# A scheduled one-core kernel: state powers in two halves, first loads in order of use, masks on either engine

## The chip, the cores and the metric

The kernel runs on one core of a Trainium2 chip. The metric is device time in microseconds; the kernel before has a median of 374.18 us over three runs (372.81 to 378.39). The engines are named as the profile names them: PE (TensorE, matrix products), PEld (its weight loads), DVE (VectorE), ACT (ScalarE), POOL (GpSimd) and SP (SyncE, which here only issues transfers). A transfer is issued on the queue of SP, ACT or POOL and carried out by 16 DMA engines.

## The reference

A block of 2048 tokens and 512 channels gets two treatments, and a gate per token mixes them.

```python
def _A_ref(x, wq, wk, wv, wo, beta):          # attention in 4 segments of 512 tokens, 32 heads of 16
    q, k, v = ...                             # x @ wq, x @ wk, x @ wv, by heads and segments
    for s in range(4):
        logits = einsum('bhqd,bhkd->bhqk', qs, ks) * scale + mask      # causal mask
        p = _softmax(logits)
        a_dot = einsum('bhqk,bhkd->bhqd', p, vs)
        num, den = phi(qs) @ M, phi(qs) @ z + 1e-06                    # memory of earlier segments
        o = g * (num / den) + (1.0 - g) * a_dot
        M, z = M + phi(ks)^T vs, z + sum(phi(ks))
    return o @ wo

def _B_ref(u, A_re, A_im, B_re, B_im, C_re, C_im, log_dt, Dskip):      # a long convolution per channel
    logdA, dB = dt * (A_re + 1j * A_im), dt * (B_re + 1j * B_im)       # 512 channels x 128 states
    P = exp(logdA[:, :, None] * l[None, None, :])                      # powers for l = 0..2047
    K = einsum('dn,dnl,dn->dl', Cc, P, dB).real
    return irfft(rfft(u) * rfft(K)) + u * Dskip

g = _sigmoid((x * gate_w).sum(-1))
return g * _A_ref(...) + (1 - g) * _B_ref(x, ...)
```

(Shortened: reshapes, casts and padding are left out.)

## The kernel before

The kernel records all its operations in a list, and a list scheduler of its own, at build time, puts them in an order for each engine, with a rough cost of each operation and a priority: a base key by stage plus an offset by tag, from a table (`ORDER`). The engines then run their fixed lists, with semaphores between them. Operations that copy a PSUM or SBUF tile (`evac`) may go to ACT or DVE, as the scheduler finds it best. All transfers, matrix products and evacuations have one line of code each (L295, L805, L302 and L303), so tiles and sizes tell them apart, not lines.

The parts that matter here:

First loads. Constants and parameters go on SP's queue; x of the first segment and the projection weights (`early`) are issued by ACT at its start.

```python
prm = (B_A_re, B_A_im, B_B_re, B_B_im, B_C_re, B_C_im)
for wi in range(6):                                  # 128 KB each, in rows of 256 bytes
    S.dma(ap(T, dims=[[128, 4], [1, 128]]), prm[wi].rearrange("(k p) n -> p k n", p=128), ..., key=0.1 * wi - 1)
S.dma(ldt, B_log_dt, ..., key=-0.9)
for T, wsrc, ky in ((wqT, A_wq, 0.3), (wkT, A_wk, 0.4), (wvT, A_wv, 0.5), (woT, A_wo, 9.0)):
    S.dma(..., 524288, w=[T], key=ky, early=ky < 1)
```

Preparation. The parameters are transposed on PE (L866), exp(dt A) is built by DVE and ACT as a real and an imaginary part, `zr` and `zi` (128 states x 512 channels, fp32).

Powers. Ten squarings give the powers 1, 2, 4, ... 512; each is stored in bf16 as re, re, im, -im, and all 512 channels are handled at once:

```python
for k in range(10):
    ACT.activation(pwT[re, re], zr, Copy)                       # L904, 128x1024
    ACT.activation(pwT[im], zi, Copy)                           # L906, 128x512
    DVE.tensor_scalar(pwT[-im], pwT[im], -1.0, mult)            # L908
    ACT: s_ = Square(zr);  d_ = Square(zi)                      # L914, L915
    DVE: ni = 2 * zr * zi                                       # L916
    DVE: nr = s_ - d_                                           # L917
    zr, zi = nr, ni
    if k == 5: ssm_cb(pb, dt)                                   # coefficients C * dt * B, 8 DVE products of 512
```

Tables. For each of four blocks of 128 channels, products of powers (L1286, L1288, L1291, DVE) build two tables, whose matrix product gives the kernel K at the exponents needed.

Attention. For each segment and group of four heads in a quarter there are five score tiles of 128x1024: score products, a causal mask, then an exponential on ACT (L1151, 160 in all). The mask is either added by one more matrix product (`negm`) before the exponential or multiplied on DVE after it (L1160); which of the two is fixed by the group:

```python
md = 8 * s + 2 * hg + gi >= MASKD            # MASKD = 24: groups 24..31 on DVE, the others on PE
...
i = mm(e, ap(PV, 128 * J, n=n, p0=32 * c, np_=17), ap(vpad[s], J * 544 + (8 * hg + hh) * 17, n=17),
       ap(pT, bk * 512 + off, n=n), ...)     # value products: 16 values and a one per head
```

Spectral stage. x is transformed in two levels, K in one (matrix products with constants), and for 16 steps the products (L1383, L1385, L1388 on DVE) and the inverse products follow. The block of a step is moved by one transfer of 256 KB into `V2`. At the end 16 products of 512 columns join the two branches, an evacuation with the gate as a scale (L305 on ACT, L306 on DVE) follows each, and the output goes out in four stores of 512 KB:

```python
for gq in range(4):
    for bl in range(4):
        pre = b4 < 4                          # the first four banks get the attention branch ahead
        ...
        S.evac(ou[bl * 512], P, 512, scale=omg4T[b4])
    S.dma(out[gq], ou, 524288)
```

Of the kernel before, what the change touches and what calls it, by code (L numbers as in the profile page):

```python
# [15 lines left out]
WIN = 3.4133  # L16
WARM = -1.0
ORDER = {
    '': (-173.582, -53.129), 'ld0': (-114.93, -18.308), 'ld1': (-97.586, 12.303), 'ld2': (-314.483, -141.787),
    'ld3': (-17.474, -40.663), 'ld4': (-139.345, 38.763), 'ld5': (-76.269, -93.461), 'ldt': (-233.997, 43.095),  # L20
    'ldw': (86.442, 71.281), 'ldc': (138.223, -52.008), 'prep': (-61.363, -40.369), 'xT': (45.662, 7.703),
    'pow0': (-321.882, -76.587), 'pow1': (-126.209, -27.757), 'pow2': (-371.748, 4.435), 'pow3': (-150.147, -151.241),
    'pow4': (-80.653, -40.547), 'pow5': (3.774, -97.638), 'cb': (-251.329, 15.495), 'pow6': (-117.016, -94.946),
    'pow7': (-462.139, 36.763), 'pow8': (-33.623, -108.583), 'pow9': (-299.842, -83.973), 'gate': (22.932, 16.612),
    'proj0.0': (-110.151, -32.513), 'tok0': (-116.048, -20.841), 'state0': (15.373, 156.393),
    'grp0.0.0': (32.669, 0.046), 'grp0.0.1': (29.753, -16.453), 'oph0.0': (63.818, -280.473),
    'proj0.1': (16.198, -92.393), 'grp0.1.0': (50.038, 50.955), 'grp0.1.1': (50.606, 0.038),
    'oph0.1': (57.101, -360.883), 'proj0.2': (-64.871, 8.032), 'grp0.2.0': (21.522, 77.803),
    'grp0.2.1': (-7.319, 72.147), 'oph0.2': (43.593, -240.036), 'proj0.3': (-113.204, -26.034),
    'grp0.3.0': (-78.183, 33.502), 'grp0.3.1': (28.034, -5.119), 'oph0.3': (-89.886, -294.08),  # L30
    'oproj0': (76.822, 66.15), 'proj1.0': (-17.113, -10.461), 'tok1': (6.274, 31.316), 'state1': (-1.66, 138.163),
    'grp1.0.0': (-244.675, -22.146), 'grp1.0.1': (-80.842, -7.868), 'oph1.0': (-51.814, -311.307),
    'proj1.1': (7.334, 23.195), 'grp1.1.0': (-94.814, 24.193), 'grp1.1.1': (83.913, -51.668),
    'oph1.1': (-151.77, -343.043), 'proj1.2': (33.686, -22.884), 'grp1.2.0': (-69.387, -48.159),
    'grp1.2.1': (-184.853, 63.024), 'oph1.2': (-146.431, -298.02), 'proj1.3': (-92.277, -78.378),
    'grp1.3.0': (-54.416, 120.304), 'grp1.3.1': (-52.668, 43.268), 'oph1.3': (-174.49, -380.844),
    'oproj1': (7.311, -29.399), 'proj2.0': (24.317, 2.404), 'tok2': (24.751, -29.031), 'state2': (-46.584, 38.683),
    'grp2.0.0': (-351.626, -1.006), 'grp2.0.1': (-94.412, 115.243), 'oph2.0': (69.419, -267.27),
    'proj2.1': (54.998, 38.92), 'grp2.1.0': (-252.693, -101.772), 'grp2.1.1': (-113.295, 30.139),
    'oph2.1': (-75.116, -437.037), 'proj2.2': (25.433, -57.215), 'grp2.2.0': (209.043, -22.16),  # L40
    'grp2.2.1': (-134.171, 67.883), 'oph2.2': (-117.243, -224.354), 'proj2.3': (217.053, -66.312),
    'grp2.3.0': (-116.791, -42.427), 'grp2.3.1': (13.259, 57.3), 'oph2.3': (143.136, -318.104),
    'oproj2': (-82.069, 10.995), 'proj3.0': (-162.313, -44.706), 'tok3': (-80.971, -45.086),
    'grp3.0.0': (-214.436, 3.177), 'grp3.0.1': (-101.384, -2.77), 'oph3.0': (40.647, -200.262),
    'proj3.1': (22.37, -26.764), 'grp3.1.0': (-25.243, 111.691), 'grp3.1.1': (-28.3, -75.051),
    'oph3.1': (-322.009, -418.76), 'proj3.2': (133.931, 42.56), 'grp3.2.0': (-51.289, -21.993),
    'grp3.2.1': (-62.933, 19.274), 'oph3.2': (153.415, -361.736), 'proj3.3': (139.126, -24.669),
    'grp3.3.0': (-204.609, 17.588), 'grp3.3.1': (-19.033, 89.621), 'oph3.3': (-9.379, -316.322),
    'oproj3': (141.911, 55.366), 'tab0': (-1.318, 68.48), 'tab1': (-14.305, 103.702), 'tab2': (17.704, 166.03),
    'tab3': (9.574, 76.971), 'xl1': (-178.257, -77.81), 'tailload': (299.499, -81.655), 'K0': (12.758, -9.76),  # L50
    'K1': (23.5, 113.643), 'K2': (-132.789, 127.457), 'K3': (-95.002, 49.886), 'K4': (-85.344, 60.314),
    'K5': (43.411, 19.376), 'K6': (39.014, 116.102), 'K7': (-22.501, 110.737), 'K8': (127.362, 73.851),
    'K9': (51.648, 57.67), 'K10': (-209.146, 67.286), 'K11': (-205.063, 112.443), 'K12': (-128.947, -8.718),
    'K13': (4.27, 178.298), 'K14': (-92.042, 99.167), 'K15': (163.434, 25.732), 'fin': (-79.92, 127.658),
    'fin0': (-437.293, 23.203), 'fin1': (-241.427, 81.848), 'fin2': (-232.803, 71.759), 'fin3': (-355.442, 133.346),
}
MASKD = 24
# [113 lines left out]
class Op:  # L171
    __slots__ = ("eng", "cost", "fn", "deps", "key", "tiles", "wt", "nd", "succ", "start", "fin", "idx", "inc",
                 "val", "sem", "know", "waits", "seq", "lat", "alld", "tag", "alts", "pen", "early", "act", "dma")


class Sched:
# [57 lines left out]
    def op(self, eng, cost, fn, r=(), w=(), pw=(), key=None, lat=None, acq=(), alts=None, act=0.0):  # L234
        o = Op()
# [6 lines left out]
        o.dma = False  # L242
        o.act = act
# [56 lines left out]
    def evac(self, dst, src, n, r, w=(), pw=(), key=None, scale=None, psum16=False, sb=False):  # L300
        if scale is None:
            fa = lambda e: e.activation(dst(), src(), ACT.Copy)  # L302
            fd = lambda e: e.tensor_copy(dst(), src())  # L303
        else:
            fa = lambda e: e.activation(dst(), src(), ACT.Copy, scale=scale())  # L305
            fd = lambda e: e.tensor_scalar(dst(), src(), scale(), None, ALU.mult)  # L306
        ex = 0.09 if scale is not None else 0.0
        return self.op("ANY", 0.0, None, r=r, w=w, pw=pw, key=key,
                       alts={"ACT": (0.17 + 0.000833 * n + ex, fa), "DVE": (0.15 + (0.00026 if sb else 0.00052 if psum16 else 0.00104) * n + ex / 2, fd)})


    def schedule(self):
# [23 lines left out]
        dma_free = 0.0  # L336
        gate = [0.0, 0.0, False]
# [12 lines left out]
        while nleft:  # L350
# [72 lines left out]
            elif e == "PE":  # L423
                left, x = o.cost, est
                while est >= gate[0] + WIN:
                    gate[2] = gate[1] > WARM * WIN
                    gate[0] += WIN
                    gate[1] = 0.0
                while left > 1e-9:
                    sp = 1.0 if gate[2] else 0.53  # L430
                    we = gate[0] + WIN
                    can = (we - x) * sp
                    d_ = min(left, can)
                    gate[1] += d_ / o.cost * o.act
                    if can >= left:
                        x += left / sp
                        left = 0.0
                    else:
                        left -= can
                        x = we  # L440
                        gate[2] = gate[1] > WARM * WIN
                        gate[0] = we
                        gate[1] = 0.0
                t[e] = x
                o.fin = x + 0.05
            else:
                t[e] = est + max(0.05, o.cost - (0.1 if e != "POOL" else 0.0))
                o.fin = est + o.cost
# [206 lines left out]
def build_kernel(nc, A_x, A_wq, A_wk, A_wv, A_wo, A_beta, B_A_re, B_A_im, B_B_re, B_B_im,  # L655
                 B_C_re, B_C_im, B_log_dt, B_Dskip, gate_w, out):
    with contextlib.ExitStack() as es:
# [20 lines left out]
        pidx = np.arange(128)  # L678
        ident = cload(np.eye(128), "ident", BF16, -2)
        mkT = cload((pidx // 16) % 2 == 1, "mk", F32, 4)  # L680
        negm = cload(np.where(pidx[None, :] < pidx[:, None], NEG, 0.0), "negm", BF16, 5)
        mask01 = cload(pidx[None, :] >= pidx[:, None], "mask01", BF16, 8)
# [3 lines left out]
        bdT = cload(bd, "bd", F32, 8)  # L686
        onesT = cload(np.ones((128, 2)), "ones", BF16, 9)
        W1T = cload(W1c, "W1", BF16, 9)
        G2T = cload(G2c, "G2", BF16, 9)
# [46 lines left out]
        vpP = mkpool("vpad", 4352, 2)  # L736
# [21 lines left out]

        a = T1
        pbP = mkpool("pb", 1024, 6, 0)  # L760
        Tp = a
        prP = mkpool("pr", 1024, 6, -1)
        a = Tp
        ftP = mkpool("ft", 2048, 7, 0)
        assert a <= T2, (a, T2)
        a = T2
        dtP = mkpool("dt", 1024, 1, 0)
        ldP = mkpool("ld", 1024, 1, 0)
        assert a <= 207 * 1024, a
# [40 lines left out]
        for wi in range(6):  # L810
            T = Tile(prP, BF16)
            S.tag = "ld%d" % wi
            S.dma(lambda T=T: ap(T, dims=[[128, 4], [1, 128]]), lambda wi=wi: prm[wi].rearrange("(k p) n -> p k n", p=128),
                  131072, w=[T], key=0.1 * wi - 1)
            praw.append(T)
        ldt = Tile(ldP, BF16)
        S.tag = "ldt"
        S.dma(lambda: ap(ldt, n=512), lambda: bass.AP(B_log_dt, 0, [[0, 128], [1, 512]]), 131072, w=[ldt], key=-0.9)
        S.tag = "ldw"
        for T, wsrc, ky in ((wqT, A_wq, 0.3), (wkT, A_wk, 0.4), (wvT, A_wv, 0.5), (woT, A_wo, 9.0)):  # L820
# [37 lines left out]
        def ssm_prep():  # L858
# [20 lines left out]
            def ft():  # L879
                return Tile(ftP, F32)  # L880
# [638 lines left out]
```

## Time and profile before

The profiled execution took 371.05 us, 369.3 us from its first to its last instruction.

| what | number |
|---|---|
| median of three runs | 374.18 us |
| PE busy | 306.9 us, 83% |
| DVE busy | 290.2 us, 79% |
| ACT busy | 288.8 us, 78% |
| granted PE clock, mean | 0.949 |
| read from HBM, written | 20.63 MB, 7.86 MB |
| 160 exponentials (L1151) | 155.7 us on ACT |
| all evacuations of PSUM and copies on ACT (L302), on DVE (L303) | 85.6 us, 69.6 us |

A row of the table of groups names line, engine, operation, the tiles and the shape of one instruction with its count, then busy time in us and the mean of one in ns, then the idle time before it and what ended it. A stretch of the table by stage gives for each engine how much of it was busy. Idle time of an engine counts only where the end waits for it.

### The profile page before, as it was taken

The numbers are of one execution on the slowest core, as the hardware profiler recorded it, in microseconds if no ns is written. First come the engines' busy times: TensorE is split into PE (matmuls) and PEld (weight loads), VectorE is DVE, ScalarE is ACT, GpSimd is POOL, SyncE is SP. The second block draws the span as 40 slices with busy tenths as digits, with TensorE's granted clock in tenths as the row PEclk, the third lists the DMA queues.
The fourth block names the chain that finished last, engine by engine and source line by source line (L and its number), as shares of the span: only waits on it lengthen the run. The fifth ranks groups of instructions, "written<-read, shape, count | busy, mean of one in ns | idle before, by whom it ended". The sixth has DMA issues, their size and how long they took to land.

```text
span 369.3 us, 8529 instructions
## 1 busy us (share of the span) xinstructions
PE 306.9 (83%) x3583; PEld 133.9 (36%) x3583; DVE 290.2 (79%) x636; ACT 288.8 (78%) x373; POOL 20.2 (5%) x38
## 2 busy tenths in 40 slices
PE   0477464998998988999888998999998999999593
PEld 0333111334444344334454343443332354434231
DVE  2268999999699998999865997389787789897310
ACT  2179999899899876888875988899868698446454
POOL 2010000000000010100300000000020200100000
PEclk9989955799999999999999999999999999999878
DMA  6910100111320135714402003000454733433414
GB/s 196 221 57 2 59 0 2 57 59 68 105 79 0 59 128 191 211 65 172 141 19 62 2 2 114 19 5 3 148 185 126 242 111 112 136 101 112 114 75 170
DMA packets 21413, 34.41 MB, mean 93 GB/s; under 512 B 8864, under 2 KB 13984, under 8 KB 20512
## 3 DMA queue, kind: packets, MB, share of 16 engines
q1 hardware_dynamic: 16112, 16.58, 14.4%
q0 software_dynamic: 3152, 15.21, 12.2%
q10 hardware_dynamic: 2112, 2.10, 1.7%
q8 instruction: 28, 0.46, 0.5%
q14 instruction: 9, 0.07, 0.1%
HBM read 20.63 MB, written 7.86 MB: 77 GB/s over the span
## 4 chain that ended last, share of the span: by engine, by line
DVE 46%; PE 30%; ACT 16%; DMA 3%; issue 2%; SPq 2%
PE psum L805 29%; DVE sb L303 9%; DVE sb L1288 8%; DVE sb L1291 7%; DVE sb L1286 6%; ACT sb L1151 5%; ACT sb L302 3%; ACT sb L305 2%; DMA sb<-in_B_A_re_dram 2%; ACT sb L904 2%; DVE sb L1198 2%; SPq L295 2%; DVE sb L1218 2%; DMA sb<-sb 1%; DVE sb L1160 1%
## 5 line engine op out<-in xcount | busy, mean ns | idle before, releaser
L805 PE MATMUL psum<-sb 128*32 128x20 bf16 (+16 forms) x3319 | 289.7, 272 | 39.3 <-ACT sb L1151 12.0
L805 PEld LDWEIGHTS psum<-sb 128*128 128x128 bf16 (+6 forms) x3319 | 117.4, 95 | 206.0 <-issue 69.2
L1151 ACT ACTIVATE sb<-psum 128x1024 bf16<-128x1024 f32 x160 | 155.7, 1030 | 8.2 <-PE psum L805 6.8
L302 ACT ACTIVATE sb<-psum 128x512 bf16<-128x512 f32 (+4 forms) x113 | 85.6, 771 | 53.3 <-PE psum L805 44.0
L303 DVE CAST sb<-psum 128x512 bf16<-128x512 f32 (+2 forms) x77 | 62.1, 813 | 15.1 <-PE psum L805 14.8
L1286 DVE TENSOR_TENSOR sb<-sb 128x512 bf16<-128x512 bf16 (+3 forms) x52 | 35.4, 683 | 0.2
L1288 DVE TENSOR_TENSOR sb<-sb 128x512 bf16<-128x512 bf16 (+3 forms) x52 | 34.5, 680 | 0.0
L1291 DVE TENSOR_TENSOR sb<-sb 128x512 bf16<-128x512 bf16 (+3 forms) x52 | 33.3, 653 | 0.2
L1160 DVE TENSOR_TENSOR sb<-sb 128x512 bf16<-128x512 bf16 (+1 forms) x40 | 14.1, 361 | 3.3 <-ACT sb L1151 3.2
L303 DVE COPY sb<-psum 128x1024 bf16<-128x1024 bf16 (+1 forms) x8 | 4.7, 582 | 13.0 <-PE psum L866 13.0
L305 ACT ACTIVATE sb<-psum,sb 128x512 bf16<-128x512 f32 x14 | 9.2, 687 | 7.0 <-PE psum L805 7.0
L866 PE MATMUL psum<-sb 128*128 128x128 bf16 x24 | 3.0, 309 | 13.9 <-DMA sb<-in_B_A_re_dram 13.9
L1388 DVE TENSOR_TENSOR sb<-sb 128x512 bf16<-128x512 bf16 x32 | 13.1, 417 | 0.4
L295 POOL DMA_DIRECT2D sb<-c_D x16 | 8.6, 538 | 87.9 <-PE psum L805 86.2
L1385 DVE TENSOR_TENSOR sb<-sb 128x1024 bf16<-128x1024 bf16 x16 | 11.0, 685 | 2.2 <-ACT sb L302 2.1
L1383 DVE TENSOR_TENSOR sb<-sb 128x1024 bf16<-128x1024 bf16 x16 | 10.8, 686 | 1.7 <-PE psum L805 1.2
L904 ACT ACTIVATE sb<-sb 128x1024 bf16<-128x1024 f32 x10 | 10.6, 1059 | 0.5 <-DVE sb L917 0.5
L1198 DVE TENSOR_TENSOR sb<-psum,sb 128x512 bf16<-128x512 bf16 x16 | 10.8, 681 | 0.0
L295 POOL DMA_DIRECT2D sb<-in_A_x_dram x7 | 4.7, 671 | 104.4 <-PE psum L848 33.5
L1190 PE MATMUL psum<-sb 128*128 128x128 bf16 x128 | 9.8, 220 | 0.5 <-DVE sb L303 0.5
L303 DVE COPY sb<-sb 128x256 bf16<-128x256 bf16 x13 | 2.8, 290 | 8.7 <-PE psum L805 8.7
L1218 DVE TENSOR_TENSOR sb<-psum,sb 128x256 bf16<-128x256 f32 x24 | 9.3, 410 | 0.2
(78 smaller groups left out, 164.7 us busy)
## 6 DMA issues: line engine op xcount, KB each, us to landing
sb<-c_D POOLq DMA_DIRECT2D x16, 320.0 KB, 3.6
scr_Z<-sb SPq DMA_DIRECT2D x16, 256.0 KB, 2.0
sb<-scr_Z POOLq DMA_DIRECT2D x4, 1024.0 KB, 5.2
sb<-sb SPq DMA_DIRECT2D x16, 256.0 KB
sb<-in_A_x_dram POOLq DMA_DIRECT2D x7, 512.0 KB, 4.5
out_dram<-sb SPq DMA_DIRECT2D x4, 512.0 KB, 3.0
scr_abuf<-sb SPq DMA_DIRECT2D x12, 128.0 KB, 1.8
sb<-scr_abuf SPq DMA_DIRECT2D x3, 512.0 KB, 4.2
```

The costliest lines, as they stand in the source:

```text
L295: o = self.op(q, 0.05 if early else issue if q == "SP" else 1.1, lambda e: e.dma_start(out(), in_(), **kw), r=r, w=w, pw=pw, key=key, lat= ...
L302: fa = lambda e: e.activation(dst(), src(), ACT.Copy)
L303: fd = lambda e: e.tensor_copy(dst(), src())
L805: mm = lambda e, o_, l, r_, st, sp, **kw: e.matmul(o_, lhsT=l, rhs=r_, start=st, stop=sp, skip_group_check=True, **kw)
L904: op("ACT", c_act(1024) + 0.04, lambda e, k=k, zr=zr: e.activation(ap(pwT[0], k * 512, [[5120, 4], [128, 2], [1, 128]]), ap(zr, 0, [[128, ...
L1151: op("ACT", c_act(1024), lambda e, P=P, pT=pT: e.activation(ap(pT, n=1024), ap(P, n=1024), ACT.Exp, scale=0.25), r=[P], w=[pT])
L1160: op("DVE", c_tt(128 * len(offs)), lambda e, pT=pT, dims=dims: e.tensor_tensor(ap(pT, dims=dims + [[1, 128]]), ap(pT, dims=dims + [[1, 128]]),
L1198: op("DVE", c_dps(512), lambda e: e.tensor_tensor(ap(o1, dims=[[128, 4], [16, 8], [1, 16]]), ap(P, dims=[[256, 4], [32, 8], [1, 16]]), ap( ...
L1218: op("DVE", c_dps(256), lambda e, hb=hb: e.tensor_tensor(ap(o2, hb * 256, [[128, 2], [16, 8], [1, 16]]), ap(P2, hb * 512, [[136, 2], [17, ...
L1286: op("DVE", c_tt(256 * n), lambda e: e.tensor_tensor(run(tile, ne, dst, 1), run(tile, ne, src, sstep), pwv(0), ALU.mult), r=rd + [pw], w=w ...
L1288: op("DVE", c_tt(256 * n), lambda e: e.tensor_tensor(run(t2, n, 0, 1), run(tile, ne, src, sstep), pwv(1), ALU.mult), r=rd + [pw], w=[t2])
L1291: op("DVE", c_tt(256 * n), lambda e: e.tensor_tensor(D_(), D_(), ap(t2, n * 128, [[-n * 128, 2], [2 * n, 64], [1, 2 * n]]), ALU.add), r=[t ...
```

## The change

It changes five things, and with them the whole table of priorities.

- Loads: all first loads go through SP's queue, each with a tag of its own, so that their order can be set by use. The parameters are read in rows of 1 KB (four channels per partition, put right by the evacuation after the transposes), x of the first segment in two halves.
- Powers: the ten squarings are done for channels 0 to 255 (A) and 256 to 511 (B) apart. Real and imaginary part lie in one tile, so one square of 512 and one copy of 512 serve both; the copies and the square may go to ACT or DVE. Half B has a later key. Coefficients are made in halves too.
- Value products write 32 columns per head instead of 17, so that the rows between are written as well; the padding is set to zero.
- Masks: a table says for each of the 160 score tiles whether PE or DVE does its mask.
- End: the last block goes in two transfers, six banks get the attention branch ahead instead of four, and the output goes out in six stores of 256 KB and four of 128 KB.

In the scheduler the model of PE's clock is dropped, and transfers are taken to begin at 4.5 us.

```diff
-MASKD = 24
+MASKS = [0, 0, 0, 0, 28, 0, 0, 31, 4, 0, 18, 20, 7, 4, 1, 0, 0, 5, 29, 26, 16, 21, 23, 0, 8, 8, 30, 30, 31, 21, 12, 8]
...  (ORDER: all offsets differ; tags for single loads and for powA0..9, powB0..9, cbA, cbB, gate0, pre0, pre1 are new)
-            S.dma(lambda T=T: ap(T, dims=[[128, 4], [1, 128]]), lambda wi=wi: prm[wi].rearrange("(k p) n -> p k n", p=128),
-                  131072, w=[T], key=0.1 * wi - 1)
+            S.dma(lambda T=T: ap(T, n=512), lambda wi=wi: prm[wi].rearrange("(p k) n -> p (k n)", k=4),
+                  131072, w=[T], key=(-1.3, -1.4, 3.0, 3.1, 3.2, 3.3)[wi])
...
-                  524288, w=[T], key=ky, early=ky < 1)
+                  524288, w=[T], key=ky)
...
+            for hb in (range(2) if s == 0 else (None,)):
+                S.dma(lambda ...: ap(xks, hb * 1024, dims=[[512, n], [1, 512]]), ...,
+                      131072 * n, w=[xp[-1]], key=(-1.2 + 0.1 * hb if s == 0 else S.key - 8), q="SP" if s == 0 else "POOL")
...
-        def ssm_powers(pb, dt, zr, zi):
+        def ssm_powers(pb, dt, z, hf):
             for k in range(10):
-                (ACT copies of 1024 and 512, DVE negation of 512)
+                S.evac(dst(128, 2), ap(z, dims=[[128, 2], [256, 2], [1, 128]]), 512, sbf=True)
+                op("DVE", c_ts4(256), tensor_scalar(dst(384, 1), dst(256, 1), -1.0, None, ALU.mult))
+                S.evac(dst(0, 1), dst(128, 1), 256, sb=True)
-                (ACT squares of 512 twice, DVE products of 512 twice)
+                op("ANY", ..., alts={"ACT": Square of 512, "DVE": tensor_tensor mult of 512})
+                op("DVE", c_f1(256), tensor_tensor(q[0:256], q[0:256], q[256:512], ALU.subtract))
+                op("DVE", c_f1(256), scalar_tensor_tensor(q[256:512], z[0:256], 2.0, z[256:512], ALU.mult, ALU.mult))
...
-            md = 8 * s + 2 * hg + gi >= MASKD
+                md = bool(MASKS[gidx] >> si & 1)
...
-                        i = mm(e, ap(PV, 128 * J, n=n, p0=32 * c, np_=17), ap(vpad[s], J * 544 + (8 * hg + hh) * 17, n=17),
+                        i = mm(e, ap(PV, 128 * J, n=n, p0=32 * c, np_=32), ap(vpad[s], J * 544 + (8 * hg + hh) * 17, n=32),
...
+                nh = 2 if t == 15 else 1          # the last block in two evacuations and two transfers
...
-                    pre = b4 < 4
+                    pre = b4 < 6
...
-                S.dma(..., lambda ou=ou: ap(ou, n=2048), 524288, r=[ou])
+                    if bl % ns == ns - 1:         # ns = 1 for the last quarter, else 2
+                        S.dma(..., 131072 * ns, r=[oup])
...
         ssm_powers(pb, dt, zz[0], 0)
+        S.key = 50.0
+        ssm_powers(pb, dt, zz[1], 1)
```

(Cut: lambdas, dependencies and pools; the pools of the preparation move, so that loads and powers get their room earlier.)

## The prediction

> **What bounds the kernel now.** I read the page's busy shares first, then a table of busy time by stage, then the timeline of the first and the last microseconds. The page says that no engine is free:
>
> ```profile
> PE 306.9 (83%) x3583; PEld 133.9 (36%) x3583; DVE 290.2 (79%) x636; ACT 288.8 (78%) x373; POOL 20.2 (5%) x38
> PEclk9989955799999999999999999999999999999878
> ```
>
> Three engines lie within 18 us of each other, so an average tells nothing. The stages do (columns: stretch, its length, busy time of each engine with instruction counts, granted clock, DMA share, GB/s):
>
> ```profile
> 0.00:20.00 20.00, 4.38 (x40) 3.62 (x40) 5.81 (x13) 5.14 (x7) 2.92 (x8) 1.00 0.74 193
> 20.00:66.00 46.00, 29.33 (x193) 11.04 (x194) 40.70 (x98) 43.35 (x67) 1.30 (x2) 0.74 0.09 31
> 66.00:124.00 58.00, 54.38 (x765) 23.58 (x764) 54.19 (x109) 53.28 (x68) 1.73 (x3) 0.97 0.15 53
> 124.00:232.00 108.00, 97.41 (x1428) 45.25 (x1426) 94.85 (x200) 89.01 (x119) 6.70 (x11) 1.00 0.30 100
> 232.00:346.00 114.00, 107.47 (x1103) 45.27 (x1103) 92.71 (x218) 87.79 (x101) 7.51 (x14) 1.00 0.34 109
> 346.00:369.00 23.00, 13.88 (x56) 5.17 (x56) 1.95 (x4) 10.26 (x16) 0.00 (x0) 0.79 0.34 125
> ```
>
> In the first 20 us everyone waits for loads. From 20 to 66 ACT (43.35 of 46) and DVE (40.70) are full while PE does 29.33 at a clock of 0.74. From 66 to 232 PE and DVE are both about 90% full. From 232 to 346 PE is (107.47 of 114), the other two have a fifth to spare. The last 23 us are a chain with nothing beside it. The chain of waits and the timeline show why the first stage is empty:
>
> ```profile
> 6.87 6.98 DMA sb<-in_B_A_re_dram
> ```
> ```profile
> 0.74 0.40 SPq L295 DMA_DIRECT2D sb<-in_B_log_dt_dram  x1
> 6.87 0.46 SPq L295 DMA_DIRECT2D sb<-in_B_A_re_dram  x1
> 13.90 2.98 PE L866 MATMUL psum<-sb 128*128 128x128 bf16 x24 [13.90 <-DMA sb<-in_B_A_re_dram]
> 17.25 1.28 DVE L877 TENSOR_TENSOR sb<-sb 128x512 f32<-128x512 bf16 x2
> 20.72 1.85 PE L805 MATMUL psum<-sb 128*128 128x512 bf16 x5 [2.44 <-DVE sb L303]
> ```
>
> The first parameter is issued tenth in SP's queue, lands at 13.9 us, and the projections wait behind all six parameter transposes until 20.72, although x and wq have landed at about 7.5 and 9.2 (issue plus time to landing).
>
> [...]from 6 to 12 us, with two issuers, the DMA share is above 1.0 at 274 to 373 GB/s, and log_dt, issued first with 128 KB, needed 5.3 us beside the 2 MB from ACT's queue. So order decides. [...]0.50 from 46 to 64 us, where PE is busy for 9.9 of 18 us, and 1.00 again from 70 us on, where it is dense.
>
> **First loads.** In the changed program SP issues A_re, A_im, ones, log_dt, ident, the two halves of x, wq, wk, wv, and then the rest. The first five are 417 KB. Data flows from about 4 us on and then at about 330 GB/s, so they are there near 6 us (log_dt alone landed at 6.07 before). Two transposes and an evacuation later, as now from 13.90 to 17.25 with six, the first DVE product can start at 8.5 instead of 17.25. x ends after 0.93 MB, near 7.5; its transposes and evacuations take some 3 us, wq is there by 9.5, and the projections start at 10.5 to 11 instead of 20.72. The mask constant needed by the first scores is now almost last, 3.2 MB into the queue, at about 14.5; but 28 projection matmuls come before the scores on PE, at 0.3 to 0.43 us about 10 us, so it is not on the path. Gain: 9 us on DVE's path, 10 on PE's; I take 9.5.
>
> **Powers in two halves.** These are the rows it removes:
>
> ```profile
> L904 ACT ACTIVATE sb<-sb 128x1024 bf16<-128x1024 f32 x10 | 10.6, 1059 | 0.5 <-DVE sb L917 0.5
> L906 ACT ACTIVATE sb<-sb 128x512 bf16<-128x512 f32 x10 | 6.2, 624 | 0.0
> L917 DVE TENSOR_TENSOR sb<-sb 128x512 f32<-128x512 f32 x9 | 6.2, 684 | 0.1
> L916 DVE SCALAR_TENSOR_TENSOR sb<-sb 128x512 f32<-128x512 f32 x9 | 6.2, 683 | 0.0
> ```
>
> ACT loses these 16.8 us and the 18 squares (11.2): 28.0. It gets 9 copies and 8 squares of 512 (0.62 each) and 12 copies of 256 (0.47, from the row of such copies): 16.2. So ACT -11.8. DVE had 6.2 + 6.2 + 2.9 (ten negations) = 15.3. It gets 18 + 18 fp32 products and differences of 256 at 0.41 (between 0.272 for 128 and 0.684 for 512 elements): 14.8; 10 squares at 0.68: 6.8; 20 negations at 0.25: 5.0; 11 copies of 512 at 0.42: 4.6; 8 of 256 at 0.29: 2.3; 33.5 in all. With the coefficients in halves (16 at 0.41 for 8 at 0.68) DVE is +19.5. The two engines together do 7 us more; what is won is that half of it comes later.
>
> **Evacuations and masks pay it back.** The scheduler moves evacuations the other way: ACT gets 13 more of 512 columns, 7 of values and 5 of transposed x, DVE loses 11, 7 and 5; of those of 1024, ACT gives up 4 and DVE takes 3. From the rows' means that is +13.7 on ACT, -13.1 on DVE. Masks multiplied on DVE go from 40 tiles to 56: 15 more at 0.418 and one at 0.277, +6.5 on DVE, and PE loses 30 mask matmuls of 256 columns[...]: -3.2. In sum ACT +2, DVE +13, PE -3. DVE also issues 62 more instructions, and back to back they start some 0.08 earlier than their durations add (0.60 apart for 0.683), so DVE's load rises by about 8.
>
> Where does it stand? Summing ACT's program in order with such durations, the 10th exponential tile has 30 us of ACT's work before it (45 before), the 60th 107 (115), the 80th 142 (141). So the early lead is repaid by the 80th tile, and past that only the start remains. On DVE the first product with the spectrum has 231 us before it (217 before): 14 more, against 9 of earlier start and some 30 us that DVE was idle between 17 us and that product (at 267 us). It fits if the schedule fills the idle time.
>
> **Value products on 32 columns.** Four of 17 columns run side by side now (390 ns for four of 512), and 32 columns move the same elements; weight loads are 94 instead of 88 ns in such rows, beside the matmuls. No time; perhaps a warmer clock early.
>
> **Last stores.** Now:
>
> ```profile
> 353.40 0.69 ACT L305 ACTIVATE sb<-psum,sb 128x512 bf16<-128x512 f32 x1 [5.16 <-PE psum L805]
> 356.58 7.83 ACT L305 ACTIVATE sb<-psum,sb 128x512 bf16<-128x512 f32 x12 [0.79 <-PE psum L805]
> ```
>
> ACT ends at 364.4, and a last 512 KB takes 3.0 us to land. A last store of 128 KB should take 1.8 (what the stores of 128 KB take), 1.2 less; the transfer of the last block in two halves gives about half a microsecond, two more prefilled banks little, as the clock is cold there. Together -2.
>
> **The sum.** -9.5 start, -2 end, -3 of masks on PE in stages where PE is nearly full, of which I count 1.5; the 8 us more on DVE are hidden but for a part, say even with a warmer clock. 374.2 - 13 = 361.
>
> **Rivals.** (1) DVE takes the place of the loads: it was full from 66 to 190 already and gets 14 us more ahead of the spectral stage. If half of the start is lost to it, the time is 367. For: its 90% in the stages from 66. Against: it now has 10 us more before 20. (2) PE eats the start: it is the bound after 232, and by the 60th tile the changed order has done less of PE's other work[...], which must follow. If its stages don't get denser, 366. (3) One queue stalls: wq, wk and wv ahead of the mask and parameter loads make first scores and powers late; the start yields 4 us only: 368. (4) The new order packs better throughout, since early PE work is no longer starved: PE at 94% from 11 us on would give 11 + 300/0.94 + 20 = 350.
>
> **Range and chances.** The rivals span 350 to 368; two of them together make 371. So 350 to 371 for 8 in 10. 2% is 366.7: faster 0.74, same 0.20, slower 0.06.
>
> **What would show it.** First DVE product near 8.5 and projections near 11; ACT less than 43 of 46 in the 20:66 stretch and PE above 36; DVE's sum near 298, ACT's near 290, PE's below 307; the last store landing in about 2 us. Wrong, if the first products come after 12 us, or if the stretch from first projection to last spectral product, 326 us now, grows by over 6.

## The result and the profile after

The changed kernel takes 362.5 us (median of four runs, 361.3 to 362.89); the kernel before, run beside it, 374.88. The ratio is 0.9655 with a 95% interval of [0.9576, 0.9734]: 3.4% faster, 1.5 us above the predicted 361.0. A ratio compares the means of the undisturbed runs of both kernels, while a median is of all runs, some of which were disturbed (of before, beside e9 to e12, one took 381.44 us at a mean clock of 0.909 and one 369.42 at 0.948). The profiled execution spans 359.5 us (before 369.3), at a mean PE clock of 0.933 (0.949).

The page's line of busy shares and its line of the granted clock, of the changed kernel:

```profile
PE 312.2 (87%) x3551; PEld 137.2 (38%) x3551; DVE 297.3 (83%) x698; ACT 289.0 (80%) x387; POOL 19.7 (5%) x42
PEclk9988869885896999999969999999999999999989
```

None of PE, DVE and ACT has less to do: against before PE is busy for 5.3 us more, DVE for 7.1, ACT for 0.2. The gain is in time that was empty. The table by stage says where (columns as in the prediction: stretch, length, busy time of PE, PEld, DVE, ACT, POOL, then clock, DMA share, GB/s):

```profile
0.00:20.00 20.00, 12.58 (x68) 6.56 (x68) 10.92 (x26) 12.62 (x19) 2.91 (x10) 1.00 0.74 219
20.00:66.00 46.00, 39.43 (x353) 16.15 (x354) 43.70 (x123) 42.69 (x61) 1.83 (x3) 0.84 0.18 58
66.00:124.00 58.00, 51.01 (x620) 22.21 (x619) 55.69 (x141) 50.31 (x79) 1.74 (x4) 0.80 0.18 54
124.00:232.00 108.00, 93.41 (x1356) 43.84 (x1355) 98.74 (x233) 92.14 (x124) 5.18 (x10) 0.97 0.22 73
232.00:346.00 114.00, 107.97 (x1126) 45.08 (x1123) 86.41 (x179) 83.32 (x98) 8.07 (x15) 0.99 0.41 125
```

In the first row each of PE, DVE and ACT does 5 to 8 us more than the 4.38, 5.81 and 5.14 of before; in the second PE does 39.43 instead of 29.33. In the third it does less (51.01 for 54.38), at a clock of 0.80 instead of 0.97. The timeline of the first microseconds, cut to the first load, the first transposes, the first DVE product and the first projections:

```profile
0.74 0.40 SPq L307 DMA_DIRECT2D sb<-in_B_A_re_dram  x1
...
5.97 1.03 PE L880 MATMUL psum<-sb 128*128 128x128 bf16 x8 [5.97 <-DMA sb<-c_ident]
...
7.65 1.28 DVE L893 TENSOR_TENSOR sb<-sb 128x512 f32<-128x512 bf16 x2
...
9.88 8.32 PE L808 MATMUL psum<-sb 128*128 128x512 bf16 x28 [1.18 <-ACT sb L314]
```

A_re is now issued at 0.74 instead of 6.87, the transposes start 7.9 us earlier (5.97 for 13.90), the product with dt 9.6 earlier, the projections 10.8 earlier. The timeline of the end, from the last inverse products (64x512) to the last evacuations:

```profile
338.93 0.63 PE L808 MATMUL psum<-sb 64*64 64x512 bf16 x8 [1.16 <-DVE sb L1417]
...
343.95 9.88 PE L808 MATMUL psum<-sb 128*128 128x512 bf16 x42 [0.27 <-DMA sb<-sb]
...
350.62 3.94 ACT L317 ACTIVATE sb<-psum,sb 128x512 bf16<-128x512 f32 x6 [0.39 <-PE psum L808]
```

The last evacuation ends at 350.62 + 3.94 = 354.56. The same instructions can be found in four kernels, the two above and the first two experiments, which makes a two-by-two table: the old or new order of first loads, with or without the rest of the change (us; e2 is the kernel before with the new loads, e1 the changed kernel with the old ones):

| landmark | before | e2 | e1 | changed |
|---|---|---|---|---|
| first projection product | 20.72 | 12.52 | 18.36 | 9.88 |
| last table products start (DVE, third of each triple) | 224.8 | 218.5 | 251.1 | 242.4 |
| first spectral product | 266.7 | 260.6 | 273.9 | 265.2 |
| last exponential starts | 310.5 | 304.4 | 315.2 | 306.5 |
| last inverse products | 346.54 | 340.49 | 347.67 | 338.93 |
| span | 369.3 | 364.4 | 368.3 | 359.5 |
| first projection to last inverse products | 325.8 | 328.0 | 329.3 | 329.1 |
| last inverse products to the end | 22.8 | 23.9 | 20.6 | 20.6 |

Read across the span: new loads are worth 4.9 in the trace without the rest and 8.8 with it. Read the two last rows: the middle is 2 to 3.5 us longer in all three changed columns, and the end is 2 to 3 shorter with the rest of the change. The middle can't be read that finely. The same order of instructions was profiled twice more, in e5 and, up to its last products, in e3, and took 332.7 and 326.8 us from first projection to last inverse products, where the table has 329.1. The profiled execution of before, 371.05 us, is also 3 us below that kernel's median. So the experiments below are judged by their timed ratios.

### The profile page after: what moved, and what is told of

It is laid out like the page before. It is cut to its first block, busy times and chain, and to the rows that moved or that the text cites. A ratio compares the mean times of both kernels' runs of the same rounds, so it can differ in the third digit from the quotient of the medians.

```text
span 359.5 us, 8560 instructions
## 1 busy us (share of the span) xinstructions
PE 312.2 (87%) x3551; PEld 137.2 (38%) x3551; DVE 297.3 (83%) x698; ACT 289.0 (80%) x387; POOL 19.7 (5%) x42
## 4 chain that ended last, share of the span: by engine, by line
DVE 43%; PE 40%; ACT 11%; issue 2%; DMA 2%; SPq 0%; DVEq 0%
PE psum L808 39%; DVE sb L1317 7%; DVE sb L1315 7%; DVE sb L315 7%; DVE sb L1320 6%; ACT sb L314 5%; ACT sb L1179 4%; DVE sb L1188 2%; DVE sb L1227 2%; DVE sb L1247 1%; ACT sb L317 1%; DMA sb<-c_ident 1%; DVE sb L1414 1%; DMA sb<-sb 1%; DVE sb L1224 1%
## 5 line engine op out<-in xcount | busy, mean ns | idle before, releaser
L808 PE MATMUL psum<-sb 128*32 128x20 bf16 (+14 forms) x3287 | 295.2, 278 | 34.1 <-ACT sb L1179 9.0
L808 PEld LDWEIGHTS psum<-sb 128*32 128x32 bf16 (+5 forms) x3287 | 119.7, 97 | 201.8 <-issue 73.0
L1179 ACT ACTIVATE sb<-psum 128x1024 bf16<-128x1024 f32 x160 | 156.5, 1036 | 11.4 <-PE psum L808 10.5
L314 ACT ACTIVATE sb<-psum 128x512 bf16<-128x512 f32 (+4 forms) x135 | 98.7, 749 | 43.8 <-PE psum L808 40.1
L315 DVE CAST sb<-psum 128x512 bf16<-128x512 f32 (+2 forms) x59 | 51.7, 883 | 12.4 <-PE psum L808 11.9
L1188 DVE TENSOR_TENSOR sb<-sb 128x512 bf16<-128x512 bf16 (+1 forms) x56 | 20.3, 376 | 3.7 <-ACT sb L1179 3.7
L1412 DVE TENSOR_TENSOR sb<-sb 128x1024 bf16<-128x1024 bf16 x16 | 10.8, 681 | 6.3 <-ACT sb L314 6.3
L314 ACT ACTIVATE sb<-sb 128x256 bf16<-128x256 bf16 (+1 forms) x30 | 14.4, 497 | 0.8 <-DVE sb L925 0.6
L1414 DVE TENSOR_TENSOR sb<-sb 128x1024 bf16<-128x1024 bf16 x16 | 10.8, 683 | 1.2 <-ACT sb L314 1.2
L1227 DVE TENSOR_TENSOR sb<-psum,sb 128x512 bf16<-128x512 bf16 x16 | 10.9, 680 | 0.0
L1219 PE MATMUL psum<-sb 128*128 128x128 bf16 x128 | 10.3, 225 | 0.4 <-ACT sb L314 0.3
L318 DVE TENSOR_SCALAR sb<-psum,sb 128x512 bf16<-128x512 f32 x3 | 2.3, 750 | 9.6 <-PE psum L808 9.5
L315 DVE COPY sb<-sb 128x256 bf16<-128x256 bf16 x19 | 4.5, 260 | 6.2 <-PE psum L808 6.2
L1219 PEld LDWEIGHTS psum<-sb 128*128 128x128 bf16 x128 | 8.2, 101 | 3.6 <-ACT sb L314 1.0
```

Source lines behind the costliest of these rows:

```text
L808: mm = lambda e, o_, l, r_, st, sp, **kw: e.matmul(o_, lhsT=l, rhs=r_, start=st, stop=sp, skip_group_check=True, **kw)
L1179: op("ACT", c_act(1024), lambda e, P=P, pT=pT: e.activation(ap(pT, n=1024), ap(P, n=1024), ACT.Exp, scale=0.25), r=[P], w=[pT])
L1188: o_ = op("DVE", c_tt(128 * len(offs)), lambda e, pT=pT, dims=dims: e.tensor_tensor(ap(pT, dims=dims + [[1, 128]]), ap(pT, dims=dims + [[1 ...
L1219: i = e.transpose(ap(P, tb * 256 + gi * 128, n=128), ap(ra[gi], tb * 128, n=128), ap(ident, n=128))
L1227: op("DVE", c_dps(512), lambda e: e.tensor_tensor(ap(o1, dims=[[128, 4], [16, 8], [1, 16]]), ap(P, dims=[[256, 4], [32, 8], [1, 16]]), ap( ...
L1414: op("DVE", c_tt(1024), lambda e, Tt=Tt, Xs=Xs, K3=K3: e.tensor_tensor(ap(Tt, dims=[[512, 2], [1, 512]]), ap(Xs, 512, [[-512, 2], [1, 512] ...
```

## Experiments

Each kernel was timed in five rounds against the kernel before on the same chip. The mean of before behind the ratios was 373.9 us beside e1 to e4, 373.4 beside e5 to e8 and 371.5 beside e9 to e12; differences of ratios are turned into microseconds with it. The three groups ran on three chips. The theory to be tested: the order of the first loads makes the gain, the end adds a little, and powers, masks and 32 columns cancel.

**e1, the changed kernel with the old order of first loads.** All programs of the engines stay; only the list of first loads is put back: constants first, A_re and A_im tenth and eleventh, x, wq, wk and wv on ACT's queue.

```diff
-SP: A_re, A_im, ones, log_dt, ident, x, x, wq, wk, wv, B_re, ... (all on SP)
+SP: log_dt, ident, mk, negm, mask, bd, ones, W1, G2, A_re, A_im, B_re, ...;  ACT: x, x, wq, wk, wv
```

> The changed kernel, every engine's program unchanged, only the first loads issued as in the kernel before: constants first on SP, A_re tenth, x, wq, wk, wv from ACT at its start. My theory: the whole lead at the start (projections at 9.9 instead of 20.7 us) comes from this order, and it goes through to the end: first DVE product at 14 to 17 us, projections at 16 to 17 (only two parameter transposes stand before x's), the time 6 to 8 us above the changed kernel's 362.5, about 369.5. Rival (the powers and the new schedule bring the gain, the loads only begin earlier into a queue of other work): below 365.

Measured: 370.08 us, ratio 0.9866 [0.978, 0.9951]. From its timeline:

```profile
14.46 1.01 PE L880 MATMUL psum<-sb 128*128 128x128 bf16 x8 [14.46 <-DMA sb<-in_B_A_im_dram]
...
18.36 4.02 PE L808 MATMUL psum<-sb 128*128 128x512 bf16 x9 [1.18 <-ACT sb L314]
```

The transposes again wait for a parameter until 14.46, and the projections start at 18.36, later than the 16 to 17 expected. Against 0.9663 for the changed kernel (e5, on another chip), the old order costs 0.0203 of 373.9 = 7.6 us; against e4, which differs from the changed kernel only in columns and ran on the same chip, 6.9. Against before, 0.9866 says that the rest of the change is worth 5.0 us [1.8, 8.2] even with the old loads.

**e2, the kernel before with the new order alone.** The opposite: nothing but the first loads differs from before, in their order and in that x and the weights move from ACT's queue to SP's.

```diff
-SP: log_dt, ident, mk, negm, mask, ..., A_re, A_im, ...;  ACT: x, wq, wk, wv
+SP: A_im, A_re, log_dt, ident, B_re, B_im, C_re, C_im, x, wq, wk, wv, mk, negm, ...
```

> The kernel before, every engine's program unchanged, only its first loads go through SP's queue alone in the order in which its engines use them: A_im, A_re, log_dt, ident, the other four parameters, x, wq, wk, wv, then constants. My theory: it starts its six parameter transposes at about 7 us instead of 13.9 and its projections at 11 to 12 instead of 20.7, so it gains 7 to 9 us: about 366.5, most of the change's 12. Rival (the gain needs the split powers, as ACT and DVE are full from 20 us on): 371 or more.

Measured: 365.44 us, 0.9772 [0.9697, 0.9847]. From its timeline:

```profile
5.33 2.35 PE L866 MATMUL psum<-sb 128*128 128x128 bf16 x20 [5.33 <-DMA sb<-c_ident]
...
12.52 4.02 PE L805 MATMUL psum<-sb 128*128 128x512 bf16 x9 [1.20 <-DVE sb L303]
```

2.3% of 373.9, 8.5 us, comes from the first loads alone, with the old masks, powers, columns and stores. This and e1 agree from both sides: about 8 of the 12 us. Order and queue change together in both, so the runs do not separate them.

**e3, the changed kernel with the old end.** One last transfer, four banks ahead, four stores of 512 KB.

```diff
-nh = 2 if t == 15 else 1;  ns = 1 if gq == 3 else 2;  pre = b4 < 6
+nh = 1;  ns = 4;  pre = b4 < 4
```

> The changed kernel with the old end: the last block in one evacuation and one transfer, four banks prefilled, four stores of 512 KB. All engines' programs are otherwise the same. My theory: the end is worth the 2.2 us by which the stretch from the last inverse products to the end of the trace shrank (20.6 for 22.8): about 364.5. Rival (the shorter end comes from the warmer PE clock there, 0.94 for 0.79, not from the stores): 363 or less.

Measured: 365.89 us, 0.969 [0.9606, 0.9775]. The last inverse products start at 336.50, the span is 359.7: 23.2 us of end instead of 20.6. The part that differs in its timeline:

```profile
342.29 11.78 PE L808 MATMUL psum<-sb 128*128 128x512 bf16 x44 [1.89 <-DMA sb<-sb]
...
346.96 7.84 ACT L317 ACTIVATE sb<-psum,sb 128x512 bf16<-128x512 f32 x12 [1.19 <-PE psum L808]
```

PE waits 1.89 us for the transfer here, 0.27 in the changed kernel, and ACT does its last twelve evacuations in a row, where in the changed kernel DVE takes one between ACT's five and its last six. The trace gives the end 2.6 us, and the other traces agree: 22.8 to 23.9 us in the three kernels with the old end, 19.7 to 20.9 in the eleven with the new one. The timed ratio is 0.003 (1 us) above that of the changed kernel with overlapping intervals, so in the timed runs the gain is not separated from zero. From the last evacuation to the span's end it is 4.9 us in before, here and in the changed kernel, though its last store of 128 KB lands in 2.1 us and the 512 KB ones in 3.0: the smaller store brought nothing that the span shows.

**e4, 17 columns again.**

```diff
-ap(PV, 128 * J, n=n, p0=32 * c, np_=32), ap(vpad[s], J * 544 + (8 * hg + hh) * 17, n=32)
+ap(PV, 128 * J, n=n, p0=32 * c, np_=17), ap(vpad[s], J * 544 + (8 * hg + hh) * 17, n=17)
```

> The changed kernel with value products on 17 columns as before; order and all else the same. My theory: four such products run side by side whatever their width, so within 1 us of 362.5, with the same cold stretches (PE clock about 0.80 from 66 to 124 us). Rival (wider products count as more activity and keep PE's clock up): the clock falls in more stretches, 3 us or more slower.

Measured: 362.84 us, 0.9682 [0.9603, 0.9762], and from 66 to 124 us a clock of 0.81 (0.80 with 32 columns). The columns do nothing, for the time or for the clock.

**e5, the changed kernel once more**, as a yardstick in five rounds for what follows. No edit.

> The changed kernel as it is, on the chip of the next three, to compare them with. Both theories: a ratio to the kernel before of 0.96 to 0.975, a cold stretch of PE between 66 and 124 us (mean clock about 0.8).

Measured: 359.95 us, 0.9663 [0.9606, 0.9719]; clock from 66 to 124 us 0.78. The cold stretch is there again.

**e6, a warmer clock.** The stretches of 6 us of the changed kernel in the cold stage (same columns as above):

```profile
80.00:86.00 6.00, 5.20 (x24) 1.78 (x20) 5.80 (x17) 5.61 (x9) 0.00 (x0) 0.50 0.00 0
86.00:92.00 6.00, 5.42 (x31) 2.55 (x32) 6.00 (x16) 5.30 (x11) 0.00 (x0) 0.50 0.00 0
```

PE is busy for 87 and 90% and yet at half clock. Part of that busy share is made by the clock: a product of 512 columns on all rows is recorded with 630 ns here and with 384 from 93 to 109 us, at full clock; where such products follow each other without a wait, they start 0.426 us apart at half clock and 0.222 at full clock (medians of 41 and 348 pairs of the same trace). The clock falls at 78.96, after 4 us in which PE does scores (on 16 or 32 of the array's 128 rows), masks and value products (on 32 of its 128 columns) and idles once for 1.05 us. Between 80 and 92 us, 19 of the 51 products that start are on the whole array with 512 columns, and 8 are scores. e6 adds 45 products on all 128 rows to the score tiles of groups 4 to 12; the scores then overwrite what they wrote.

```diff
+if 4 <= gidx <= 12:
+    mm(e, ap(P, n=n), ap(ident, n=128), ap(qT, n=n), True, True)      # n = 512 - 128 * J
```

> The changed kernel with 45 more matrix products: one ahead of each score tile of groups 4 to 12, with all 128 rows of PE at work, into the bank that the tile's first product then overwrites. Order and all else the same[...]. My theory (the stretch after the first projections did not get shorter because PE runs at half clock from 80 to 94 and from 109 to 116 us, as score products use only 16 of 128 rows): clock at least 0.95 from 66 to 124, and in spite of the work the same time or up to 4 us faster. Rival (DVE sets the pace there, the clock follows from it and costs nothing): no faster, and slower by up to 8 us.

Measured: 364.18 us, 0.9704 [0.9639, 0.9769]. Its stage from 66 to 124:

```profile
66.00:124.00 58.00, 48.96 (x637) 22.15 (x643) 55.49 (x141) 51.35 (x79) 1.74 (x4) 0.97 0.17 54
```

The clock goes from 0.80 to 0.97, and the time does not improve. PE's cold clock is real, but its cure, at the price of 45 more products, brings no gain that these runs show. In this stage DVE is at 55.49 of 58 (55.69 with the cold clock), which fits.

**e7, no mask work on DVE.** The 56 multiplications by the mask are cut to 4 columns each, so those tiles stay unmasked, and their exponentials are then as good as ready for the value products.

```diff
-ap(pT, dims=dims + [[1, 128]]), ap(pT, dims=dims + [[1, 128]]), ap(mask01, ...), ALU.mult)
+ap(pT, n=4), ap(pT, n=4), ap(mask01, n=4), ALU.mult)
```

> The changed kernel, but the 56 mask multiplications on DVE are cut to 4 columns of each row (so those tiles stay unmasked): some 11 us less of DVE's work, same instructions, same order. Theory of the clock: DVE is not what holds the middle, within 2 us of the changed kernel. Rival (DVE's 7 us more are what eats the gain of PE and ACT): 5 us or more faster.

Measured: 355.02 us, 0.9439 [0.937, 0.9509], 8.4 us below e5 by the ratios (0.0224 of 373.4), 4.9 by the medians. From its page:

```profile
PE 304.5 (86%) x3523; PEld 137.1 (39%) x3551; DVE 286.4 (81%) x698; ACT 288.6 (82%) x387; POOL 19.8 (6%) x42
```

DVE's sum falls by 10.9 to 286.4. The table products end 6 us earlier (last start 236.0 for 242.4), the first spectral product comes at 258.6 for 265.2, the last inverse products at 332.22 for 338.93: nearly all of it is won before the spectral stage. My forecast of no more than 2 us fell, and the rival's of 5 or more came true. That DVE's load is the reason is not shown by this run alone, as a tile's value products then also wait less long for its mask step.

**e8, no mask work on PE.** The 208 mask products of the other 104 tiles are left out (the score products then end their sums themselves), those tiles stay unmasked.

```diff
-for bk in (() if md else range(2)):
+for bk in ():
```

> The changed kernel without the 208 mask products on PE (so those 104 tiles stay unmasked): about 17 us of PE's work less[...], else the same. If PE is what holds the stretches from 66 us on, 6 us or more faster; if the lighter load turns PE's clock down, or DVE and ACT hold the middle, less than 3.

Measured: 366.11 us, 0.9724 [0.966, 0.9787]. From its page:

```profile
PE 304.4 (83%) x3316; PEld 130.8 (36%) x3343; DVE 298.6 (82%) x698; ACT 288.8 (79%) x387; POOL 19.8 (5%) x42
PEclk9879655685655899969559995798999999999998
```

Less work on PE, and no gain. The clock is 0.63 and 0.64 in the stages from 20 and from 66 us, 0.82 from 124 to 232; the 512-column score products on 16 rows take 473 ns instead of 391. The mean clock was 0.812 to 0.860 in all six runs, against 0.904 to 0.932 in e5's on the same chip. What was taken off PE came back as a slower clock.

**e9 and e10, masks moved back to PE.** 35 of the 56 tiles masked on DVE are in groups 0 to 23, 21 in groups 24 to 31. e9 moves the 35 to PE, e10 all 56; the order of the programs is kept (a multiplication of 4 columns, 0.156 us, stays on DVE in each place), and nothing of the computation is left out.

```diff
-def f(e, P=P, ent=ent, md=md):
+def f(e, P=P, ent=ent, md=md and gidx >= 24):        # e10: >= 32; the multiplication on DVE is cut to n=4 for these tiles
```

> The changed kernel with the 35 DVE masks of groups 0 to 23 given back to PE as matrix products; the DVE instructions stay in their places but touch 4 columns that are masked already, so the output is the same and the order too. About 8 us less on DVE, 6 us more on PE, all in the stretch in which DVE is full and PE's clock falls. Theory after the last runs (DVE holds the middle at about half a microsecond of time per microsecond of its work, PE's work there is nearly free as it keeps its clock up): 3 to 5 us faster than the changed kernel, a ratio of about 0.955 to the kernel before. Rival (what the run without DVE masks won came from DVE's relief in the last third, where these masks don't lie, or PE's work costs as much as DVE's saves): within 1 us of the changed kernel, 0.966.

> The same for all 56 DVE masks: 11 us less on DVE, 10 us more on PE, the last 21 of them in groups 24 to 31, beside the stage in which PE is full. Theory: those 21 gain nothing or cost up to 3 us, so this one is slower than or like the run with 35. Rival (only DVE counts): faster than that by 2 us.

Measured: e9 358.11 us, 0.9662 [0.9603, 0.9721]; e10 364.59 us, 0.9818 [0.9759, 0.9877]. Within some 3 us, the early masks are worth the same on either engine: DVE's sum falls by 6.0, PE's rises by 3.2, the time stays. The 21 late ones are not: on PE they cost 0.0156 of 371.5 = 5.8 us. The stage from 232 to 346 us, e9 and then e10:

```profile
232.00:346.00 114.00, 108.13 (x1120) 45.12 (x1109) 85.96 (x178) 83.62 (x99) 8.05 (x15) 0.99 0.41 125
```

```profile
232.00:346.00 114.00, 109.93 (x1151) 46.70 (x1149) 81.18 (x176) 83.09 (x97) 8.06 (x15) 0.99 0.42 125
```

DVE has 28 us to spare in that stage and PE 6; the first spectral product comes 1.8 us later in e10, the last inverse products almost 4 later, so about half of that arises ahead of the spectral products.

**e11, half of the cost that halved powers put on DVE.** The 36 fp32 products and differences of the two halves on 64 columns instead of 256 (the powers are then incomplete), which takes 6.3 us off DVE.

```diff
-tensor_tensor(f32(q, 0, 256), ...);  scalar_tensor_tensor(f32(q, 256, 256), ...)
+tensor_tensor(f32(q, 0, 64), ...);   scalar_tensor_tensor(f32(q, 256, 64), ...)
```

> The changed kernel with the 36 products and differences of the powers on 64 columns instead of 256 (the powers are then not those of the reference): about 7 us less of DVE's work before 115 us, same instructions, same order. Theory (DVE holds everything from 20 to 230 us, so what the halved powers add to DVE is paid): 3 to 4 us faster than the changed kernel. Rival (the powers lie beside work of ACT and their load on DVE is hidden; masks alone cost): within 1 us.

Measured: 359.71 us, 0.9659 [0.958, 0.9738]: the same as e5. In its trace the first spectral product comes 4.5 us earlier than in the changed kernel (260.7 for 265.2) and the end 2.7; the same order with the full products gave 262.7 (e3) and 269.2 (e5), so this is hardly outside the spread. The intervals leave room for some 3.6 us either way: the 3 to 4 us expected are unlikely but not ruled out, the whole 6.3 are.

**e12, half B early.** The second half's key goes from 50 to 6, so that both halves are asked for at the start, as all channels were in the kernel before.

```diff
-S.key = 50.0
+S.key = 6.0
```

> The changed kernel with the powers of half B asked for as early as those of half A (base key 6 instead of 50). The scheduler makes its whole order anew for this, so only a large difference says something. Theory (putting half of the powers off is what lets exponentials and tables begin early while ACT and DVE are full): 3 us or more slower. Rival (it does not matter when they come): within 2 us.

Measured: 376.54 us, 1.0121 [1.0051, 1.0191], PE's sum 330.4 at a clock of 0.62 from 20 to 66 us and 0.72 from 66 to 124 (in the profiled execution, the slowest of its six with 380.77 us). By the ratios that is 17 us more than the changed kernel, but the key makes the scheduler place everything anew with a table of priorities tuned for the other key. It shows that this table depends on half B being late; it does not say what being late is worth by itself.

## Why the prediction was right, step by step

**First loads: right, and the whole mechanism.** Predicted 8.5 for the first DVE product and 10.5 to 11 for the projections, measured 7.65 and 9.88. Predicted gain 9.5, measured 10.84 at the projections in the trace. Of these the loads bring 8.5 (9.88 for 18.36 in e1) or 8.2 (12.52 for 20.72 in e2), and the time shows 7.6 and 8.5: that part of the lead is kept. The other 2.4 are the rest of the change: in e1, with the old loads, 8 transposes of parameters stand ahead of the projections instead of 24. The estimate took the 417 KB ahead of the transposes to decide, not the number of queues. The trace of before alone does not show that; e2 gets its 8.5 us with one issuer less for these loads than before. One figure was off without harm: the mask constant, issued at 13.46, takes 4.8 us to land and is there near 18.3, not at 14.5. No wait for it is recorded, as the first score products start at 18.36, behind the projections, but nothing was to spare.

**The middle: predicted -1.5, +3.2 between the two traces.** This is the step that failed; its size in time stays open. The timed medians differ by 12.4, which leaves +0.6 for it beside 10.8 of the start and 2.2 of the end, and traces of one order spread over 6 us here. What failed for certain is the term of 3.2 us less on PE with "a warmer clock": PE's sum was to stay below 307 and is 312.2, because the same products took longer. The 3.2 were my estimate for 30 mask products of 256 columns, at a rate that the trace of before does not show: where products of this shape follow each other there without a wait, they start 0.122 us apart at full clock (median of 85 pairs), which would make 3.7. The stage from 66 to 124 ran at 0.80 instead of 0.97. The rows by shape show it in the largest group, before and then after, beside the halved powers:

```profile
L805 PE MATMUL psum<-sb 128*128 128x512 bf16 x496 | 129.9, 398 | 14.9 <-DVE sb L303 5.3 <-DMA sb<-sb 3.2 <-DVE sb L1061 2.2
...
L808 PE MATMUL psum<-sb 128*128 128x512 bf16 x496 | 137.5, 415 | 11.4 <-ACT sb L314 4.3 <-DMA sb<-sb 2.0 <-DVE sb L1087 1.9
...
L934 DVE TENSOR_TENSOR sb<-sb 128x256 f32<-128x256 f32 x18 | 7.5, 416 | 0.0
L935 DVE SCALAR_TENSOR_TENSOR sb<-sb 128x256 f32<-128x256 f32 x18 | 7.5, 415 | 0.0
```

I had taken PE's clock in before (0.50 from 46 to 64 us, with PE busy for 9.9 of the 18) to follow the busy share of the profile, which was no more than an estimate. The traces say that this share does not show it. Nor did the fall at 78.96 need a stretch without work: in the 3.41 us ahead of it PE was busy for 2.17. In the six traces that record every product, all 39 slow stretches that begin after 10 us and end within the span last a whole number of steps of 3.41 us, so one can ask what PE did in each step. PE was over 99% busy in 32 of the 39 last steps, after which the clock came back, but also in 25 of the 53 others. What divides them better is how much of the array the products filled, rows times columns, with 0.427 us for 512 columns at half clock (as such products start apart in the trace of before): 61% or more in the last steps, at most 77% in the others, and a limit at 76% puts 85 of the 92 right. In the traces of before and the changed kernel alone, with a product counted to the step in which it starts, it is 78% or more in the 11 last steps and at most 75% in the 13 others. Rows alone do not divide them. e6 and e8 fit, with 45 full products added and 208 left out. It is a reading of traces; no run changed the filled share alone.

The second term, "the 8 us more on DVE are hidden but for a part", stays open. DVE rose by 7.1 as predicted. In e7, 10.9 us less of it gave 5 to 8, but there the step between exponential and value product also becomes shorter; e9 and e11 say that 6 us less on DVE, traded for PE work or taken from the powers alone, give nothing clear. Nor does the two-by-two table say which part of the change lengthens the middle: it is 2.2 us longer with the new loads alone, 3.5 with the rest alone and 3.2 with both, all within the spread. That a longer PE sum costs time is not shown either, as e6 with a warm clock is no faster.

**Powers, evacuations, masks: right in their sums.** Busy time ACT +0.2 and DVE +7.1 (predicted +8), durations added up ACT +2.7 (+2) and DVE +14.7 (+13), products of 256 at 0.416 and 0.415 (0.41), ACT 42.69 in the stretch from 20 to 66 (under 43), PE 39.43 there (over 36). They change the order a lot and the end little: table products end 24 us later than in e2, the first spectral product comes 4.6 later, and the stretch from there to the last inverse products is 6.2 us shorter (73.7 for 79.9), with PE busy for 71.0 us of it instead of 74.2 and DVE for 61.4 instead of 67.3.

**32 columns: right**, nothing that the time or the clock shows (e4); the hoped-for warmer clock did not come.

**The end: right in size by luck, wrong in its make-up.** -2.2 in the trace for -2 predicted. The term of 1.2 for the smaller last store is zero (4.9 us after the last evacuation in all three kernels). Of before, the lines are:

```profile
346.54 0.63 PE L805 MATMUL psum<-sb 64*64 64x512 bf16 x8 [1.14 <-DVE sb L1388]
...
352.32 0.13 PEld L805 LDWEIGHTS psum<-sb 128*128 128x128 bf16 x2 [0.94 <-DMA sb<-sb]
```

From the last inverse products to the last transfer it is 5.0 us instead of 5.8 (338.93 to 343.95, before 346.54 to 352.32; 5.8 again in e3), so the split transfer brings 0.8, predicted 0.5; from there to the end of the last evacuation 10.6 instead of 12.1. For those 1.5 there are two candidates that I did not separate, the banks filled ahead and the clock, 0.86 before and 0.94 now in that stretch. In e3, with the old end, that stretch takes 12.5 us at a clock of 0.83: both went back together. In the timed runs the end isn't separated from zero.

**The sum.** In the traces: -10.8 start, +3.2 middle, -2.2 end, -9.8 together; the timed medians differ by 12.4. By the ratios the loads are worth 7.6 to 8.5 us and all the rest 4.1 (from e2 to the changed kernel) to 5.0 (e1), about what the 2.4 of the start and the 2.2 of the end add up to. Rivals 1 and 2, by which DVE or PE takes back a part of the start, are not borne out by that, nor excluded; rival 3 is refuted by 9.88 and 18.36, rival 4 by the time.

**Left open.** The kernel before masked all 40 tiles of groups 24 to 31 on DVE, the changed one only 21. By e10 a late mask on PE costs 5.8 / 21 = 0.28 us, so the 19 moved to PE may cost some 5 us; to put them back on DVE, and to leave early ones on PE, was not tried. None of the kernels that compute the whole reference is faster than the changed one; e9 equals it.

## What to carry over

Order first loads by first use and count the bytes ahead of each first use; with all of them on one queue, that was worth 2.3% here. What it is worth to move work between engines differed by stage: the same mask made no measured difference on either engine early and cost 0.28 us on PE late, where PE had 6 us to spare and DVE 28. Before counting on less PE work as gain, look at the clock that it leaves behind: 0.829 instead of 0.933 with 208 products fewer.

## What the runs showed of the hardware that I had not expected

- PE is at half clock (0.50) for 12 us while the profile has it busy for 5.2 and 5.4 of each 6 us; 45 products on all 128 rows lift that stage from 0.80 to 0.97.
- The clock changes in steps of 3.41 us: the slow stretches of the changed kernel that begin between 24 and 342 us last 3.41, 6.8 or 13.65 us, the long one of before 23.9. Each ended with a step in which the products filled 78% of the array or more (at 0.427 us for 512 columns), and busy time does not show that: PE was busy for all of the step from 51.95 us in before too, with 59% filled, and the clock stayed at half after it.
- 208 products fewer on PE lower its mean clock from 0.933 to 0.829, and PE's busy time falls by 7.8 us only, of which a part is that 27 of the 3343 products have no record in that trace.
- A last store of 128 KB lands 0.9 us sooner than one of 512 KB, and the span ends no sooner after the last evacuation: 4.9 us with either.
